# Two k multiplications moved to VectorE, the first expert's number found without a queue, row scatters begun a turn earlier

## The chip, the cores and the metric

The kernel runs on one core of a Trainium2 chip. The metric is the device time of one execution in microseconds (us); for the kernel before it is given as the median of three runs. The engines are TensorE (PE; its weight loads are PEld), VectorE (DVE), ScalarE (ACT), GpSimd (POOL) and the queue of SyncE (SP), which issues most DMAs. Each engine works through its own instructions in order.

## The reference

The computation is a gated linear attention followed by a mixture of experts, in float32. There are 4 sequences of 768 tokens, 8 heads of width 48, hence 3072 tokens of width 384.

```
f = sigmoid(f_logit)
for t in range(768):                                  # per sequence and head
    state = f[t][:, None] * state + outer(k[t], v[t])
    y[t] = q[t] @ state
x = y as 3072 rows of 384
e = argmax(x @ w_gate);  g = softmax(x @ w_gate)[e] * sigmoid(x @ w_output_gate)[e]
out = g * (relu(x @ w1[e]) @ w2[e])                   # 8 experts, hidden width 1024
```

## The kernel before, in words

**Attention in turns.** The recurrence is cut into chunks of 128 tokens: 4 sequences by 6 chunks give 24 chunks, worked off in 24 turns `t` (loop at line 465). Within a chunk the decay is turned into a running product p and its inverse i: `scan_p` (line 212) and `scan_i` (219) are scans along the chunk on VectorE. k is multiplied by i (`mul_k`, 223), q by p (`mul_q`, 226). Then the chunk is plain matrix work: `qk` (248) gives the scores of q and k, `mask` makes them causal, one half by a copy on ScalarE and a selection on POOL (253, 254), the other by a multiplication with a mask on VectorE (257); `out_y` (308, 312) adds what the state before the chunk gives and what the masked scores give; `state` (281) and `state_upd` (293 to 296) carry the state on. `evac_y` (319) copies the output out of PSUM as the tile xt, `x_tr` (325) transposes it and takes the gate logits along.

The turns overlap: turn `t` does the scores of chunk t, `mul_k` of chunk t + 1, the scans and `mul_q` of chunk t + 2, the output of chunk t - 1, and the copy, the transpose and the state update of chunk t - 2. `mul_k` and `mul_q` are POOL's, but for `mul_k` of the first three chunks, which is VectorE's (line 195). The order on each engine is that in which the loop issues the instructions; nothing sorts them afterwards.

**Routing beside it.** The 24 chunks of tokens fall into groups (four of 4, then four of 2). For each group `route` (367) puts eight small VectorE instructions into a list, `dq`; `fill` takes some from it at fixed places of each turn (eight a turn up to turn 19, more from turn 20), so that they stand between the large ones. When they are through, `slots` (406) runs with the next turn: a few small matmuls rank the tokens, and VectorE writes the slot of each token (419, 421). From turn 8 (`T_SCAT`, line 527) each turn ends with `scatter`: an indirect DMA, issued by POOL, that writes 128 token rows to their experts' slots in the buffer xs_dram; one a turn up to turn 19, up to four in turn 20. That buffer's upper slots are first cleared by eight SP DMAs (668); the first two scatters may overtake these, the later ones wait for them.

**The first expert.** After 16 chunks have been counted, in turn 19, `top` (392) finds the expert with the most tokens. Its first instruction (396) runs at once; the other six, the last of them the SP load of that expert's number and of its first weights (`ex.load`, 402, 403, 619), go to the front of `dq`: four of them come in turn 19, two in turn 20. When 16 row blocks have been scattered, at the end of turn 20, SP reads the first 256 rows of that expert back (`tokens_in`, 675) and then its second weights (634).

**Handing over.** In turn 22 the buffers of the early chunks are given up and the experts' weight tiles take their place (`done_sb.close()`, line 481). ScalarE and POOL begin to split the weights into a high and a low part (`split`, 649, 650). In turn 23 `x_early` (754) transposes the 256 early rows, after the last turn `mm1_early` (806) starts the expert, and then the eight experts follow one after the other, the largest first, with the next one's weights and rows loading beside them.

Of the kernel before, what the change touches and what calls it, by code (L numbers as in the profile page):

```python
# [14 lines left out]
ALU = mybir.AluOpType  # L15
AX = mybir.AxisListType
# [4 lines left out]
N, DM, E, F = B * S, H * D, 8, 1024  # L21
# [20 lines left out]
RW = LG + 2 * E  # L42
RG = (4, 4, 4, 4, 2, 2, 2, 2)
XW = 2 * D + 2 * E
T_SCAT = 8
HELD = 256
SB = 32
BW = DM // (128 // SB)
# [81 lines left out]
def attention(ctx, tc, nc, k, kpool, rt, q01, k01, f01, q23, k23, f23, v, wg, xs_dram, r, ex):  # L130
# [60 lines left out]
    def prep(ti):  # L191
        b, c = order[ti]
        i, sl, z = b % 2, slice(c * C, (c + 1) * C), ti % 2
        flat = lambda a: a.rearrange("p g t -> p (g t)")
        eng = nc.vector if ti < 3 else nc.gpsimd
        d = {}

        def s():
# [37 lines left out]
    def hot(t):  # L236
        return 0 <= t < len(order)
# [113 lines left out]
    dq, pq = [], []  # L351
# [40 lines left out]
    def top(ps):  # L392

        key = rt.tile([128, E], F32, name="key")
        mx = rt.tile([128, 1], F32, name="mx")
        nc.vector.scalar_tensor_tensor(out=key, in0=ps, scalar=float(E), in1=k.first_key, op0=ALU.mult, op1=ALU.add)
        dq[:0] = [
            lambda: nc.vector.tensor_reduce(out=mx, in_=key, axis=AX.X, op=ALU.max),
            lambda: nc.vector.tensor_tensor(out=r.top, in0=key, in1=mx.broadcast_to([128, E]), op=ALU.is_equal),
            lambda: nc.vector.tensor_tensor(out=key, in0=r.top, in1=k.num, op=ALU.mult),  # L400
            lambda: nc.vector.tensor_reduce(out=mx, in_=key, axis=AX.X, op=ALU.add),
            lambda: nc.vector.tensor_copy(out=r.top_id, in_=mx),
            lambda: ex.load(0, r.top_id[0:1, 0:1], rest=False),
        ]

    def slots(gi, t0, n):
        ts = slice(t0, t0 + n)
# [21 lines left out]
    for i in range(2):  # L429
        nc.sync.dma_start(out=turn[64 * i:64 * i + 64, 1::2, 2 * D:XW],  # L430
                          in_=wg[64 - 64 * i:128 - 64 * i, 1::2, 0:2 * E])
# [5 lines left out]
    def pre(t, *names):  # L437
        if hot(t):
            for nm in names:
                if nm not in done[t]:  # L440
                    done[t].add(nm)
                    pre_of[t][nm]()
# [8 lines left out]
    for g in range(2):  # L451
        for j in range(2):
            r0 = 64 * (j ^ g)
            nc.gpsimd.tensor_copy(out=turn[:, g::2, D * j:D * j + D],
                                  in_=k.ident[:, r0:r0 + D].unsqueeze(1).broadcast_to([128, 2, D]))
# [9 lines left out]
    for t in range(last + 1):  # L465
# [10 lines left out]
            state_upd(t - 2)  # L476
        if t == 2:
            pre(4, "f")
        pre(t + 1, "mul_k")
        if t + 1 == last:  # L480
            done_sb.close()
            ex.open_early()
        fill(more)
        if t > 1:
            pre(t + 2, "scan_p")
        qk(t)
        mask(t, 1)
        mask(t, 0)
        if t == 0:
            pre(2, "s", "f")  # L490
        pre(t + 2, "scan_p", "scan_i")
        if t == 0:
            pre(2, "mul_k")
# [24 lines left out]
        if t == last:  # L518
# [7 lines left out]
            ex.split(1, 0, 2, nc.gpsimd)  # L526
        if t >= T_SCAT:
            scatter(1 if t < T_END else 2)
# [701 lines left out]
```

## Time and profile before

| | |
|---|---|
| median of three runs | 366.68 us (364.68, 366.68, 368.03) |
| profiled execution | 361.12 us |
| its span, first to last instruction | 359.4 us |
| granted TensorE clock, mean | 1.000 of full speed |
| PE, DVE, ACT, POOL busy | 343.4, 259.4, 183.2, 146.8 us |

A row of a timeline gives the start in us from the span's start, the duration in us, the engine, the line, the instruction, output<-input, and in brackets how long the engine was idle before it and what released it. Rows of other views are explained where they stand. `L223` is line 223 of the kernel; SPq is the SP queue. The chunks' scores (L248) mark the turns: those of turn 21 start at 103.67 us.

### The profile page before, as it was taken

How to read it: one execution, taken by the hardware profiler on the slowest of the kernel's cores; microseconds unless marked ns; L12 is line 12 of the kernel's file. 1: busy time of each engine (PE TensorE's matmuls, PEld its weight loads, DVE VectorE, ACT ScalarE, POOL GpSimd, SP SyncE). 2: the span in 40 equal slices, each digit the busy share in tenths (PEclk: the TensorE clock that was granted, in tenths of full speed). 3: DMA queues.
4: the chain of work that ended last, by engine and by line, in shares of the span. 5: the costliest groups of instructions: out<-in, count | busy, mean ns of one | idle time of the engine just before them, and what ended most of it. 6: DMA issues, size and time to landing. Idle time of an engine off the chain costs nothing. (4 is left out here: it accounts for less than half of the span.)

```text
span 359.4 us, 8283 instructions
## 1 busy us (share of the span) xinstructions
PE 343.4 (96%) x3001; PEld 317.6 (88%) x3001; DVE 259.4 (72%) x517; ACT 183.2 (51%) x436; POOL 146.8 (41%) x176
## 2 busy tenths in 40 slices
PE   7889999999996999999999999999999999999994
PEld 2678898888896799997999899999999999999993
DVE  6998989898994665576685884975975974966610
ACT  3476776776763743455542453452552552464510
POOL 7586786999988853022000005004005005007112
PEclk9999999999999999999999999999999999999999
DMA  8999999999528714999458298399498499192101
GB/s 256 350 359 355 347 241 262 286 281 233 213 92 254 262 47 138 218 266 257 131 169 135 51 330 249 54 290 282 79 293 249 96 321 278 35 288 81 42 24 43
DMA packets 81458, 74.02 MB, mean 206 GB/s; under 512 B 37058, under 2 KB 76037, under 8 KB 81408
## 3 DMA queue, kind: packets, MB, share of 16 engines
q1 hardware_dynamic: 78096, 63.76, 63.8%
q0 software_dynamic: 3312, 9.65, 7.7%
q8 instruction: 25, 0.41, 0.5%
q14 instruction: 25, 0.20, 0.2%
HBM read 57.16 MB, written 16.68 MB: 205 GB/s over the span
## 5 line engine op out<-in xcount | busy, mean ns | idle before, releaser
L885 POOL DMA_INDIRECT out<-yr,dst x20 | 21.5, 1074 | 133.8 <-DMA yr<-yd 86.3
L810 ACT ACTIVATE hh<-h_ps 128x256 fp32r<-128x256 f32 (+6 forms) x72 | 34.8, 484 | 66.7 <-PE h_ps L806 65.2
L806 PE MATMUL h_ps<-xh,w1h 128*128 128x400 f32 (+6 forms) x192 | 66.9, 348 | 0.9 <-DVE hl L811 0.7
L811 DVE SCALAR_TENSOR_TENSOR hl<-h_ps,hh 128x256 fp32r<-128x256 f32 (+6 forms) x72 | 38.8, 540 | 37.8 <-ACT hh L810 37.2
L806 PE MATMUL h_ps<-xl,w1h 128*128 128x400 f32 (+6 forms) x192 | 65.1, 339 | 0.2 <-DVE xl L761 0.2
L806 PE MATMUL h_ps<-xh,w1l 128*128 128x400 f32 (+6 forms) x192 | 64.9, 338 | 0.0
L825 PE MATMUL y_ps<-hh,w2h 128*128 128x400 f32 (+3 forms) x120 | 42.2, 352 | 0.0
L825 PE MATMUL y_ps<-hh,w2l 128*128 128x400 f32 (+3 forms) x120 | 42.1, 351 | 0.0
L825 PE MATMUL y_ps<-hl,w2h 128*128 128x400 f32 (+3 forms) x120 | 42.1, 351 | 0.0
L806 PEld LDWEIGHTS h_ps<-xh,w1h 128*128 128x128 f32 x192 | 36.0, 188 | 6.3 <-DVE hl L811 4.7
L806 PEld LDWEIGHTS h_ps<-xl,w1h 128*128 128x128 f32 x192 | 36.1, 188 | 0.9 <-DVE xl L761 0.5
L806 PEld LDWEIGHTS h_ps<-xh,w1l 128*128 128x128 f32 x192 | 36.1, 188 | 0.4
L226 POOL TENSOR_TENSOR q_t<-q_t,p 128x512 f32<-128x512 f32 x24 | 30.6, 1274 | 8.4 <-DVE p L212 5.8
L248 PE MATMUL a_ps<-q_t,k_t 64*128 64x128 f32 x384 | 28.3, 285 | 5.8 <-POOL k_t L223 2.8
L650 DVE TENSOR_TENSOR w2l<-w2r,w2h 128x768 fp32r<-128x768 f32 x31 | 30.6, 989 | 3.5 <-ACT w2h L649 1.8
L248 PEld LDWEIGHTS a_ps<-q_t,k_t 64*128 64x128 f32 x384 | 23.6, 187 | 8.6 <-POOL k_t L223 3.4
L212 DVE TENSOR_TENSOR_SCAN p<-f_ps,start_p 128x511 f32<-128x511 f32 x22 | 28.0, 1274 | 3.7 <-ACT start_p L200 2.1
L650 DVE TENSOR_TENSOR w1l<-w1r,w1h 128x768 fp32r<-128x768 f32 x28 | 26.8, 956 | 3.5 <-ACT w1h L649 2.7
L223 POOL TENSOR_TENSOR k_t<-k_t,i 128x512 f32<-128x512 f32 x21 | 26.9, 1280 | 4.2 <-DVE i L219 2.7
L219 DVE TENSOR_TENSOR_SCAN i<-f_ps,start_i 128x512 f32<-128x512 f32 x22 | 26.9, 1223 | 0.8
L325 PE MATMUL x_ps<-turn,xt 128*128 128x112 f32 x192 | 25.7, 277 | 1.7 <-ACT xt L319 1.7
L649 ACT CAST w1h<-w1r 128x768 fp32r<-128x768 f32 x32 | 26.0, 834 | 2.3 <-POOL k_t L223 2.3
(175 smaller groups left out, 764.2 us busy)
## 6 DMA issues: line engine op xcount, KB each, us to landing
w1r<-in_w SPq DMA_DIRECT2D x32, 384.0 KB, 5.1
w2r<-in_w SPq DMA_DIRECT2D x32, 384.0 KB, 4.5
xs_dram<-empty SPq DMA_DIRECT2D x8, 401.0 KB, 9.7
f_t<-in_f SPq DMA_DIRECT2D x6, 512.0 KB, 7.2
q_t<-in_q SPq DMA_DIRECT2D x6, 512.0 KB, 8.9
k_t<-in_k SPq DMA_DIRECT2D x6, 512.0 KB, 9.6
v_t<-in_v SPq DMA_DIRECT2D x6, 512.0 KB, 8.7
v_t<-in_v SPq DMA_DIRECT2D x4, 768.0 KB, 14.2
```

What stands on the lines that cost most here:

```text
L212: nc.vector.tensor_tensor_scan(out=flat(d["p"])[:, 1:n], data0=flat(d["f"])[:, 0:n - 1], data1=sp[:, 1:n], initial=sp[:, 0:1], op0=ALU.mul ...
L219: nc.vector.tensor_tensor_scan(out=flat(d["i"])[:, ::-1], data0=flat(d["f"])[:, ::-1], data1=flat(k.start_i[z])[:, ::-1], initial=0.0, op0 ...
L223: eng.tensor_tensor(out=k_t[i][:, :, sl], in0=k_t[i][:, :, sl], in1=d["i"], op=ALU.mult)
L226: nc.gpsimd.tensor_tensor(out=q_t[i][:, :, sl], in0=q_t[i][:, :, sl], in1=d["p"], op=ALU.mult)
L248: nc.tensor.matmul(aps[t][par][:, g, :], k_t[b % 2][r, g, sl], q_t[b % 2][r, g, sl], start=(g == 0), stop=(g == NP - 1))
L325: nc.tensor.matmul(xps[t][:, g, :], xt[t][:, g, :], turn[:, g, :], start=(g == 0), stop=(g == NP - 1))
L649: self.nc.scalar.copy(out=flat(hi), in_=raw)
L650: (eng or self.nc.vector).tensor_tensor(out=flat(lo), in0=raw, in1=flat(hi.bitcast(F32)), op=ALU.subtract)
L806: nc.tensor.matmul(ps[:, 0:n], a[:, c, cs], b, start=(i == 0), stop=(i == 3 * KC - 1))
L810: nc.scalar.activation(out=hi, in_=ps[:, 0:n], func=AF.Relu)
L811: nc.vector.scalar_tensor_tensor(out=lo, in0=ps[:, 0:n], scalar=0.0, in1=hi.bitcast(F32), op0=ALU.max, op1=ALU.subtract)
L825: self.nc.tensor.matmul(self.yps[d][:, 0:n], a[:, d, fs], b, start=(f == 0 and i == 0), stop=(f == KF - 1 and i == 2), skip_group_check=True)
```

## The change

Three edits. From `T_VEC` = 22 on, `mul_k` (of chunks 22 and 23, issued in turns 21 and 22) is VectorE's, and it is issued behind the turn's mask instead of ahead of the scores; in those turns the forward scan is issued behind it too. In `top` the six instructions no longer go through `dq` but follow at once, so they stand ahead of the slot computation of the same group. `T_SCAT` becomes 7.

```diff
@@ -42,7 +42,8 @@
 RW = LG + 2 * E
 RG = (4, 4, 4, 4, 2, 2, 2, 2)
 XW = 2 * D + 2 * E
-T_SCAT = 8
+T_SCAT = 7
+T_VEC = 22
 HELD = 256
 SB = 32
 BW = DM // (128 // SB)
@@ -192,7 +193,7 @@
         b, c = order[ti]
         i, sl, z = b % 2, slice(c * C, (c + 1) * C), ti % 2
         flat = lambda a: a.rearrange("p g t -> p (g t)")
-        eng = nc.vector if ti < 3 else nc.gpsimd
+        eng = nc.vector if ti < 3 or ti >= T_VEC else nc.gpsimd
         d = {}
 
         def s():
@@ -394,14 +395,12 @@
         key = rt.tile([128, E], F32, name="key")
         mx = rt.tile([128, 1], F32, name="mx")
         nc.vector.scalar_tensor_tensor(out=key, in0=ps, scalar=float(E), in1=k.first_key, op0=ALU.mult, op1=ALU.add)
-        dq[:0] = [
-            lambda: nc.vector.tensor_reduce(out=mx, in_=key, axis=AX.X, op=ALU.max),
-            lambda: nc.vector.tensor_tensor(out=r.top, in0=key, in1=mx.broadcast_to([128, E]), op=ALU.is_equal),
-            lambda: nc.vector.tensor_tensor(out=key, in0=r.top, in1=k.num, op=ALU.mult),
-            lambda: nc.vector.tensor_reduce(out=mx, in_=key, axis=AX.X, op=ALU.add),
-            lambda: nc.vector.tensor_copy(out=r.top_id, in_=mx),
-            lambda: ex.load(0, r.top_id[0:1, 0:1], rest=False),
-        ]
+        nc.vector.tensor_reduce(out=mx, in_=key, axis=AX.X, op=ALU.max)
+        nc.vector.tensor_tensor(out=r.top, in0=key, in1=mx.broadcast_to([128, E]), op=ALU.is_equal)
+        nc.vector.tensor_tensor(out=key, in0=r.top, in1=k.num, op=ALU.mult)
+        nc.vector.tensor_reduce(out=mx, in_=key, axis=AX.X, op=ALU.add)
+        nc.vector.tensor_copy(out=r.top_id, in_=mx)
+        ex.load(0, r.top_id[0:1, 0:1], rest=False)
 
     def slots(gi, t0, n):
         ts = slice(t0, t0 + n)
@@ -476,18 +475,22 @@
             state_upd(t - 2)
         if t == 2:
             pre(4, "f")
-        pre(t + 1, "mul_k")
+        late = t + 1 >= T_VEC
+        if not late:
+            pre(t + 1, "mul_k")
         if t + 1 == last:
             done_sb.close()
             ex.open_early()
         fill(more)
-        if t > 1:
+        if t > 1 and not late:
             pre(t + 2, "scan_p")
         qk(t)
         mask(t, 1)
         mask(t, 0)
         if t == 0:
             pre(2, "s", "f")
+        if late:
+            pre(t + 1, "mul_k")
         pre(t + 2, "scan_p", "scan_i")
         if t == 0:
             pre(2, "mul_k")
```

## Rows read from the trace of the kernel before

**Rows 1.** The page, busy time, share and instructions of each engine
```profile
PE 343.4 (96%) x3001; PEld 317.6 (88%) x3001; DVE 259.4 (72%) x517; ACT 183.2 (51%) x436; POOL 146.8 (41%) x176
```

**Rows 2.** Windows view, 105 to 125 us: length, then busy us of each engine
```profile
105.00:125.00 20.00, 16.44 (x257) 14.04 (x256) 11.62 (x37) 11.00 (x27) 17.13 (x18) 1.00 0.78 254
```

**Rows 3.** TensorE's timeline, turns 21 to 23: start, us, instruction, idle before it
```profile
103.67 1.16 PE L248 MATMUL a_ps<-q_t,k_t 64*128 64x128 f32 x16
110.48 1.16 PE L248 MATMUL a_ps<-q_t,k_t 64*128 64x128 f32 x16 [1.94 <-POOL k_t L223]
116.06 1.16 PE L248 MATMUL a_ps<-q_t,k_t 64*128 64x128 f32 x16 [0.88 <-POOL k_t L223]
117.47 1.15 PE L325 MATMUL x_ps<-turn,xt 128*128 128x112 f32 x8 [0.25 <-ACT xt L319]
120.70 0.63 PE L754 MATMUL x_ps<-ident,first_x 128*128 128x128 f32 x4
```

**Rows 4.** POOL's timeline, turns 19 to 22
```profile
99.95 1.01 POOL L342 DMA_INDIRECT xs_dram<-xn,slot  x1 [0.17 <-issue]
100.99 1.28 POOL L223 TENSOR_TENSOR k_t<-k_t,i 128x512 f32<-128x512 f32 x1
108.15 0.98 POOL L342 DMA_INDIRECT xs_dram<-xn,slot  x1 [0.30 <-issue]
109.14 1.28 POOL L223 TENSOR_TENSOR k_t<-k_t,i 128x512 f32<-128x512 f32 x1
114.73 1.28 POOL L223 TENSOR_TENSOR k_t<-k_t,i 128x512 f32<-128x512 f32 x1
```

**Rows 5.** Source view, line 223 on VectorE: count, ns min/median/max, first and last
```profile
L223 DVE TENSOR_TENSOR k_t<-k_t,i x3: 692/692/1040, 8.4 to 15.5; 128x512 f32<-128x512 f32 x3
```

**Rows 6.** VectorE's timeline, turns 19 to 22
```profile
99.55 0.19 DVE L421 TENSOR_REDUCE slot<-rk 128x4 int32<-128x32 f32 x1
103.70 0.13 DVE L402 CAST top_id<-mx 128x1 int32<-128x1 f32 x1
107.15 0.66 DVE L257 TENSOR_TENSOR at<-a_ps,mask 128x512 f32<-128x512 f32 x1
109.74 0.36 DVE L296 TENSOR_TENSOR state<-misc,pend 128x192 f32<-128x192 f32 x1
```

**Rows 7.** ScalarE's timeline, turn 22
```profile
109.26 0.37 ACT L319 COPY xt<-two_ps 128x256 f32<-128x256 f32 x1 [0.46 <-DVE rk L419]
```

**Rows 8.** SP queue's timeline, first token read of expert 0
```profile
115.18 0.37 SPq L675 DMA_DIRECT2D first_x<-xs_dram  x1
```

**Rows 9.** DMA view, 100 to 130 us: issues, KB each, us to landing
```profile
first_x<-xs_dram SPq DMA_DIRECT2D x1, 401.0 KB, 4.0
```

**Rows 10.** VectorE's timeline, turn 7
```profile
45.54 0.19 DVE L421 TENSOR_REDUCE slot<-rk 128x4 int32<-128x32 f32 x1
```

**Rows 11.** POOL's timeline, turn 10
```profile
59.50 1.27 POOL L226 TENSOR_TENSOR q_t<-q_t,p 128x512 f32<-128x512 f32 x1 [2.57 <-DMA q_t<-in_q]
```

**Rows 12.** TensorE's weight loads, timeline, turn 14
```profile
72.00 0.97 PEld L248 LDWEIGHTS a_ps<-q_t,k_t 64*128 64x128 f32 x16 [0.18 <-POOL k_t L223]
```

**Rows 13.** DMA view, 40 to 70 us: queue, packets, MB, share of 16 engines
```profile
q0 software_dynamic: 192, 0.62, 6.2%
```

**Rows 14.** VectorE's timeline, 124 to 137 us
```profile
125.02 1.99 DVE L650 TENSOR_TENSOR w2l<-w2r,w2h 128x768 fp32r<-128x768 f32 x1
135.19 0.96 DVE L650 TENSOR_TENSOR w2l<-w2r,w2h 128x768 fp32r<-128x768 f32 x1 [0.30 <-ACT w2h L649]
```

**Rows 15.** POOL's timeline, 120 to 137 us
```profile
124.33 1.85 POOL L650 TENSOR_TENSOR w1l<-w1r,w1h 128x768 fp32r<-128x768 f32 x1
134.94 0.98 POOL L342 DMA_INDIRECT xs_dram<-xn,slot  x1 [0.30 <-issue]
```

**Rows 16.** Tile view of the clearing writes: issues, and time to landing
```profile
L668 SPq DMA_DIRECT2D xs_dram<-empty x8: 372/686/1049, 32.5 to 39.9; - x8
DMA to landing us min/median/max: 9.2/9.7/12.2
```

## The prediction

> **What bounds the kernel now.** The page comes first: TensorE is busy 96% of the span and POOL 41% [rows 1]. A mean over stages does not price an edit in one stage, so the second view is the window in which the change ends, 105 to 125 us. There TensorE is busy 16.44 of 20 us and POOL 17.13 [rows 2]: 3.56 us of TensorE idle lie here, and that is the most that these edits can take out of this stretch. TensorE's timeline names the waits [rows 3]. The scores of turn 22 start at 110.48 after 1.94 us of idle, those of turn 23 at 116.06 after 0.88 us, both released by POOL's multiplication of k (line 223); the transpose of turn 21's output at 117.47 waits 0.25 us for xt. POOL's timeline says why k is late [rows 4]: POOL does nothing wrong, it is simply queued up. The last of turn 20's four scatters starts at 108.15, the multiplication of k of chunk 22 directly behind it at 109.14, that of chunk 23 at 114.73. From then on TensorE has work nearly without a gap, so what arrives earlier there should end earlier.
>
> **Moving the last two multiplications.** POOL loses two instructions of 1.28 us [rows 4]; VectorE gains two at 0.69 us, the usual duration of the same line in the first turns, at most 1.04 [rows 5]. Is k ready in time there? The forward scan of chunk 23 now stands behind the mask and the multiplication, so the mask of turn 21, which began at 107.15 behind that scan [rows 6], begins about 1.2 us sooner, at 105.96, and k of chunk 22 is done at about 105.96 + 0.6 + 0.69 = 107.25. TensorE could start that turn's scores at 110.48 - 1.94 = 108.54 [rows 3], so the whole 1.94 us go. Everything that follows on VectorE in turn 21 is 0.6 us later: the state update that began its last step at 109.74 and took 0.36 [rows 6] ends at 110.7 instead of 110.1. Behind it come the mask (0.6, its input long there) and the second multiplication (0.69): k of chunk 23 is done at about 112.0. Its scores want it at 116.06 - 1.94 - 0.88 = 113.24, so the 0.88 us go as well, and so does the 0.25 us of 117.47: xt was late there because ScalarE sat behind a weight cast that waited for POOL's multiplication.
>
> What is late next: ScalarE's copy of xt at 109.26 was held until VectorE's rank multiplication of that turn was over [rows 7]. That one is 0.6 us later now, so xt is there near 110.3, while TensorE is through with the transposes of k at about 110.1. I charge 0.25 us. Sum of this part: 1.94 + 0.88 + 0.25 - 0.25 = 2.82 us gained.
>
> **The expert's number in one go.** Five small VectorE instructions, about 0.2 us each by the slot reduction's 0.19 [rows 6], stand ahead of the ranks of turn 19 instead of behind them; only the cast (0.13) truly moves, from 103.70 to about 100.3, so VectorE's total is the same. The slots of that group, ready at 99.55 + 0.19 = 99.74 [rows 6], are ready at about 100.7. That costs POOL a wait, because turn 19's scatter is now the first row block of just this group: it starts at about 100.9 instead of 99.95 [rows 4]. Behind it in POOL's queue stands k of chunk 21 (100.99 before), now done at about 103.2; TensorE wants it at 103.67 [rows 3]. Cost nothing, with 0.45 us to spare; if the wait is longer than that, the rest is lost. On the SP queue the expert's weights start some 3.3 us sooner, into DMA engines that were nearly idle then, and nothing else stands behind them in that queue until turn 20 ends.
>
> **Scatters from turn 7.** The number of scatters is the same, 24, each one place earlier, so three instead of four stand in turn 20. POOL's last one there is 0.93 later by the wait above and one step of 0.98 + 0.30 = 1.28 us earlier [rows 4]: start 107.8 instead of 108.15. The read of the early tokens waits for it. That read went out at 115.18 [rows 8] and took 4.0 us [rows 9], so tokens lay at 119.2, and the transposes that use them began at 120.70 [rows 3]. With TensorE 2.8 us earlier they begin at 117.9, and the tokens would be late if nothing moved. But the scatters then shared the DMA engines with the expert's weights; these are now 3.3 us ahead. I put the read near 112 and the tokens near 116: covered.
>
> At the front the extra scatter of turn 7 must wait for its slots (45.54 + 0.19 [rows 10]), so POOL starts it near 45.9, just where the multiplication for the next turn stood; POOL then runs about 1.3 us late for three turns. That is hidden: POOL sits 2.57 us at 59.50 anyway, waiting for a load of q [rows 11]. The load itself is the cost. Up to 72.00, where TensorE's weight load of the scores waits for POOL's k [rows 12], POOL works from that load without a rest, so what delays the load delays TensorE. A scatter costs the 16 DMA engines 6.2% of 30 us over three of them, 0.62 us each [rows 13], in a stretch in which they are full, and about one scatter more now goes ahead of that load. Bounds: 0, if it slips into idle engines, and 1.24, if both of the first two go ahead of it. A gain isn't to be had, since the load has no less ahead of it. I take 0.6, one scatter.
>
> **The sum.** 2.82 - 0.6 = 2.2 us off. The profiled execution took 361.12 us (its span of 359.4 and 1.7 around it), so its like would take 358.9. The runs' median, 366.68, lies 5.56 us above that execution; the gain is a difference inside the span, so I take it off the median: 364.5 us, 0.6% less.
>
> **A rule against it.** The trace shows that a VectorE instruction with both inputs in SBUF can be held by POOL: a subtraction of 0.96 us [rows 14] took 1.99 when a POOL subtraction had begun before it and ran to 126.18 [rows 14, 15]. Beside a POOL scatter it does not: the one at 135.19 took 0.96 although a scatter ran until 135.92 [rows 14, 15]. The new multiplications have both inputs in SBUF, and by POOL's queue only scatters run beside them, so I charge nothing. The Trainium skill, page "SBUF — State Buffer", section "Who interferes with whom", states that such an instruction and a GpSimd instruction that reads SBUF exclude each other for a whole instruction; the trace agrees (1.99 against 0.96), and if it held for scatters too, each multiplication could come a scatter late and the result would be the third rival's.
>
> **Rivals.**
> - *Nothing lost at the front, and the stretch closes up* (0.16). For it: later turns have slack on POOL. Against it: the 0.18 us wait at 72.00. The bound is all 3.56 us of idle: 363.1.
> - *The early tokens are the new wait* (0.08). If their read goes out after 113.9 instead of 112, TensorE waits for them. At worst they lie where they lay, 119.2, and 1.3 of the 2.2 us are given back: 365.8.
> - *VectorE becomes the bound of turns 21 to 23* (0.14). It carries 1.4 us more there. If a multiplication is held by a POOL scatter or multiplication (about 1 us), everything behind it, rank and xt among them, is 1 us later and xt's wait grows by as much: 365.5.
> - *The third scatter waits for the clearing writes* (0.05, slower than before). Only the first two may overtake them; the third moves from turn 10 to turn 9, near 54.8. The last clear was issued at 39.9 and the longest landing is 12.2, so 52.1 at worst in this execution [rows 16]. Were it later, POOL would stand with k of chunk 11 queued behind the scatter. Of the 2.57 us that POOL has to spare at 59.50 [rows 11], 1.3 are used by turn 7's wait, so TensorE loses what goes beyond 54.8 + 1.3 = 56.1, and the gain is used up from a landing at 58.3. A landing at 62 gives a loss of 3.7: 370.4.
> - *The change does not do what it says* (0.07): the scores of turn 22 find another releaser at the same time, q of that chunk or the score buffers, both on engines just as full. No change: 366.7.
>
> The forecast has the remaining 0.50.
>
> **How the numbers follow.** About 1% (3.7 us) is what a measurement of this kernel can tell from no change; the runs shown spread from 364.68 to 368.03. Faster by over 1% means below 363.0. The forecast gets there by scatter of the median alone (about 0.18 of its cases), the first rival in half of its cases, the others seldom: 0.09 + 0.08 + 0.03 = 0.20. Slower by over 1% (above 370.3) is the rival of the clearing writes and a little of the rest: 0.06. Within 1%: 0.74. The range reaches from 0.9 us below the first rival, for the scatter of the runs, to just above the case of no change: 362.2 to 367.0. The slower rival and the tails of the others are left out.
>
> **What the trace after would show.** Right: the k multiplication five times on VectorE, the last two near 107 and 111; scores of turns 22 and 23 without a wait for k; the cast of the expert's number about 3 us earlier; the first scatter near 46; the first token read near 112. Wrong: a wait of over 0.5 us before the scores of turn 21, before the token transposes, or TensorE more than 1 us later at turn 15 than before; or a POOL scatter in turn 9 released by the clearing writes.

## The result, and the profile after

The whole change takes **360.86 us** (median; 359.25 to 361.26) where the kernel before, measured beside it, takes 365.0 us (362.85 to 368.03, the three runs shown among them): ratio 0.989, 95% interval 0.986 to 0.992. The forecast was 364.5, with a range from 362.2 to 367.0. The sign is right; the change is worth 4.1 us instead of 2.2, and the time lies below the range. Medians and ranges, here and below, are of all runs; the ratios and their intervals leave out runs over 1.5% above the fastest of the same kernel, and can differ from the quotient of the medians by a few tenths of a percent.

One thing is odd at once. The profiled execution of after took 361.26 us, its slowest run, and that of before 361.12, faster than any of its timed runs. The two profiled executions differ by 0.1 us, the medians by 4. So two questions stand: does the late stretch win what was forecast, and what do the ordinary executions of the kernel before lose that its profile does not show?

The page of after and its window from 105 to 125 us answer to [rows 1] and [rows 2]:

```profile
PE 344.4 (96%) x3001; PEld 317.9 (88%) x3001; DVE 260.7 (73%) x519; ACT 183.3 (51%) x436; POOL 144.4 (40%) x174
```

```profile
105.00:125.00 20.00, 19.06 (x304) 16.51 (x305) 14.97 (x45) 12.20 (x31) 16.66 (x18) 1.00 0.73 251
```

Two instructions have gone from POOL to VectorE, and TensorE is busy 19.06 of 20 us instead of 16.44. Its timeline in turns 21 to 23, against [rows 3]:

```profile
106.35 1.16 PE L249 MATMUL a_ps<-q_t,k_t 64*128 64x128 f32 x16
111.88 1.16 PE L249 MATMUL a_ps<-q_t,k_t 64*128 64x128 f32 x16
116.51 1.16 PE L249 MATMUL a_ps<-q_t,k_t 64*128 64x128 f32 x16
117.60 1.15 PE L326 MATMUL x_ps<-turn,xt 128*128 128x112 f32 x8
120.84 0.63 PE L757 MATMUL x_ps<-ident,first_x 128*128 128x128 f32 x4
```

The waits of 1.94, 0.88 and 0.25 us have gone. (One of 0.39 us is new, at 111.73 ahead of a rank matmul; the profile names no releaser for it, and e8, e11 and e12 below do not have it.) From the scores of turn 21 to the token transposes it takes 14.49 us instead of 17.03: 2.54 us won. But turn 21 itself starts 2.68 us later than before (106.35 against 103.67), which eats it. POOL's and VectorE's timelines, against [rows 4] and [rows 6], and the source view of line 224 on VectorE, against [rows 5]:

```profile
46.11 1.22 POOL L343 DMA_INDIRECT xs_dram<-xn,slot  x1 [1.17 <-DVE state L294]
...
54.97 1.01 POOL L343 DMA_INDIRECT xs_dram<-xn,slot  x1 [0.17 <-issue]
...
103.18 1.01 POOL L343 DMA_INDIRECT xs_dram<-xn,slot  x1 [1.50 <-DVE state L294]
104.22 1.29 POOL L224 TENSOR_TENSOR k_t<-k_t,i 128x512 f32<-128x512 f32 x1
```

```profile
101.84 0.17 DVE L399 TENSOR_TENSOR top<-key,mx 128x8 f32<-128x8 f32 x1
102.04 0.17 DVE L400 TENSOR_TENSOR key<-top,num 128x8 f32<-128x8 f32 x1
...
102.43 0.15 DVE L402 CAST top_id<-mx 128x1 int32<-128x1 f32 x1
...
102.72 0.19 DVE L420 TENSOR_REDUCE slot<-rk 128x4 int32<-128x32 f32 x1
...
109.00 0.68 DVE L224 TENSOR_TENSOR k_t<-k_t,i 128x512 f32<-128x512 f32 x1
...
113.79 0.68 DVE L224 TENSOR_TENSOR k_t<-k_t,i 128x512 f32<-128x512 f32 x1
```

```profile
L224 DVE TENSOR_TENSOR k_t<-k_t,i x5: 682/693/1042, 8.4 to 113.8; 128x512 f32<-128x512 f32 x5
```

The SP queue, against [rows 8]:

```profile
103.64 2.18 SPq L622 DMA_DIRECT2D w1r<-in_w  x4
113.67 0.37 SPq L678 DMA_DIRECT2D first_x<-xs_dram  x1
```

Two k multiplications stand on VectorE, at 109.00 and 113.79, and the read of the early tokens goes out 7.3 us behind the start of turn 21 instead of 11.5. The step to read is at 103.18 on POOL: POOL's scatter of turn 19 now waits 1.50 us, where before it went at once [rows 4]. The profile names the state update as what released it, but it starts 0.27 us behind the end of its slots (102.72 + 0.19 on VectorE), and in each of the six further profiles with scatters from turn 7 it starts 0.27 or 0.28 us behind them: it waits for the slots. The 2.7 us that turn 21 is late come from the front (2.2 us) and from turn 20 (0.5 us). These are TensorE's two largest waits at the front, at turns 12 and 13, and a copy of ScalarE in turn 20:

```profile
64.88 1.23 PE L249 MATMUL a_ps<-q_t,k_t 64*128 64x128 f32 x16 [0.60 <-POOL k_t L224]
...
72.71 0.44 PE L313 MATMUL two_ps<-at,v_t 128*64 128x128 f32 x4 [0.90 <-DMA v_t<-in_v]
```

```profile
102.77 0.37 ACT L320 COPY xt<-two_ps 128x256 f32<-128x256 f32 x1 [0.59 <-DVE rk L418]
```

TensorE waits for a k of POOL and for a load of v that both came in time in the profile of before. In turn 20 ScalarE's copy of xt waits for VectorE's rank multiplication, which now stands behind the small instructions of the expert's number.

### The profile page after: what moved, and what is told of

Read it like the earlier page. It is cut to its first block, busy times and chain, and to the rows that moved or that the text cites. A ratio compares the mean times of both kernels' runs of the same rounds, so it can differ in the third digit from the quotient of the medians.

```text
span 359.6 us, 8283 instructions
## 1 busy us (share of the span) xinstructions
PE 344.4 (96%) x3001; PEld 317.9 (88%) x3001; DVE 260.7 (73%) x519; ACT 183.3 (51%) x436; POOL 144.4 (40%) x174
## 5 line engine op out<-in xcount | busy, mean ns | idle before, releaser
L343 POOL DMA_INDIRECT xs_dram<-xn,slot x24 | 24.2, 1010 | 7.7 <-issue 3.8
L838 PE MATMUL y_ps<-w2h,hh 128*128 128x384 f32 (+1 forms) x80 | 27.1, 339 | 0.0
```

The lines of the kernel that those rows point to most:

```text
L343: i = nc.gpsimd.indirect_dma_start(out=xs_dram, out_offset=bass.IndirectOffsetOnAxis(ap=r.slot[:, t:t + 1], axis=0), in_=xn[t // 4][:, t % ...
L838: self.nc.tensor.matmul(ps[0:n, 0:DM], a, b[:, f % 2, :], start=(f == 0 and i == 0), stop=(f == KF - 1 and i == 2))
```

## The experiments

Each ratio is to the kernel before, measured beside the run (medians of before: 363.2 for e1 to e4, 363.3 for e5 to e8, 363.0 for e9 to e12, 364.6 for e13 to e15). "Turn 20" is the time between the scores of turns 20 and 21 in the profile, 4.63 us where nothing waits, as before (99.04 to 103.67). "Held" is explained below.

| run | scatters from | multiplications / number | median us (range) | ratio, 95% | v late | held | turn 20 |
|---|---|---|---|---|---|---|---|
| e1 | 8 | POOL / queue | 363.1 (361.7 to 367.5) | 1.000 [0.996, 1.004] | no | no | 4.64 |
| e2 | 8 | VectorE / queue | 360.5 (358.9 to 363.2) | 0.993 [0.990, 0.996] | 0.83 | yes | 5.83 |
| e3 | 8 | POOL / in one go | 363.1 (361.7 to 366.8) | 1.000 [0.996, 1.005] | 1.53 | yes | 6.85 |
| e4 | 7 | POOL / queue | 361.2 (360.0 to 362.4) | 0.994 [0.991, 0.997] | no | no | 4.64 |
| e5 | 7 | VectorE / queue | 359.4 (358.6 to 363.5) | 0.991 [0.988, 0.994] | 0.78 | no | 4.63 |
| e6 | 8 | VectorE / in one go | 361.1 (358.9 to 364.5) | 0.993 [0.990, 0.997] | 1.69 | yes | 8.40 |
| e7 | 8 | e2, PSUM operands | 362.4 (361.2 to 364.2) | 0.998 [0.995, 1.001] | 1.73 | no | 4.63 |
| e8 | 7 | whole change, v early | 361.1 (359.4 to 362.7) | 0.993 [0.990, 0.996] | no | no | 5.12 |
| e9 | 8 | e6, PSUM operands | 361.5 (361.1 to 365.2) | 0.996 [0.993, 1.000] | no | no | 5.35 |
| e10 | 8 | e6, v early | 360.0 (358.5 to 363.9) | 0.993 [0.989, 0.997] | no | yes | 8.35 |
| e11 | 7 | e5 again | 358.9 (358.4 to 360.7) | 0.989 [0.984, 0.993] | no | no | 4.64 |
| e12 | 7 | whole change again | 359.6 (359.2 to 366.2) | 0.989 [0.983, 0.994] | 1.04 | no | 5.14 |
| e13 | 8 | e6, VectorE 0.4 later | 366.5 (362.6 to 370.4) | 1.002 [0.998, 1.006] | no | yes | 8.41 |
| e14 | 7 | whole change, VectorE 0.4 later | 360.0 (359.8 to 361.3) | 0.988 [0.983, 0.993] | no | no | 5.52 |
| e15 | 8 | before, VectorE 0.4 later | 364.9 (363.9 to 366.4) | 1.002 [1.000, 1.005] | no | yes | 5.94 |

**The kernel before, again (e1).** No edit.

> The kernel before, unchanged, for a second profile. Its profiled execution so far (361.12 us) is faster than each of its six timed ones (362.85 to 368.03, median 365.0). Theory 1, a wait that comes and goes: a second execution near 365 shows TensorE idle some 3 to 4 us longer in one stretch than the first profile, and it is the stretch of turns 8 to 15, where the DMA engines are full and loads land late. Theory 2: the excess is at turns 20 to 23, the first tokens read back too late, and the first token read goes out after 117. Theory 3: the excess is spread over the whole span, or lies outside it, and no stretch differs by over 1 us.

Its runs spread over 5.8 us, with a tail to 367.5, and its profiled execution is again its fastest run (361.65), so it decides between none of the three theories. It shows no wait for v, and TensorE's wait for k is there (1.78 us at 110.66). Behind that wait TensorE's granted clock fell from 1.00 to 0.50, the lower of its two levels (1.2 instead of 2.4 GHz), and stayed there from about 111 to 114.5 us; turn 22 took 6.22 us instead of 5.58. The profile of before has a wait as long (1.94 us) and no such fall. One profile of this kernel is no picture of its median.

**One edit at a time (e2, e3, e4).** The multiplications alone (with their place in the order), the number alone, the scatters alone:

```diff
# e2
-        eng = nc.vector if ti < 3 else nc.gpsimd
+        eng = nc.vector if ti < 3 or ti >= T_VEC else nc.gpsimd
...
# e3
-        dq[:0] = [
-            lambda: nc.vector.tensor_reduce(out=mx, in_=key, axis=AX.X, op=ALU.max),
...
+        nc.vector.tensor_reduce(out=mx, in_=key, axis=AX.X, op=ALU.max)
...
# e4
-T_SCAT = 8
+T_SCAT = 7
```

> Only the last two k multiplications on VectorE behind the mask; the queue of small instructions and the scatters as before. By the prediction's terms this part is worth 2.8 us (ratio 0.992) and the waits of 1.94 and 0.88 us for k in turns 22 and 23 are gone. Theory 2 of the run before (tokens read back late) wants less here, since the read of the tokens isn't earlier: under 1.5 us (0.996 or above), with a wait before the token transposes.

> Only the first expert's number found in one go. By the prediction: no gain and no loss (ratio 1.000 within 0.003), since the waits for k in turns 22 and 23 stay; weights of the first expert issued near 101.6 instead of 104.9. If the weights' earlier start is what takes the load off the scatters and the token read (theory 2), the ratio is 0.996 or less.

> Only the scatters from turn 7. By the prediction: TensorE loses 0.6 us (0 to 1.24) at turns 10 to 14, and gains up to 1.28 us at turn 22 since three scatters instead of four stand ahead of its k multiplication: together 0.7 us faster (ratio 0.998). If the early scatter brings nothing in the front and the gain at turn 22 stays, 0.9965; if the front loses what the two profiles differ by there (2.7 us), 1.004 or above.

e2 wins 0.73% (2.7 us): the late part of the forecast. e3 wins nothing. e4 wins 2.1 us, where the forecast had a loss of 0.6 for this edit beside the others, and the expectation a gain of 0.7 for it alone. Part of that is plain in TensorE's timeline of e4:

```profile
109.28 1.16 PE L248 MATMUL a_ps<-q_t,k_t 64*128 64x128 f32 x16 [0.72 <-POOL k_t L223]
```

With one scatter less ahead of it in turn 20, POOL's k of chunk 22 comes 1.2 us sooner (0.72 us of wait instead of 1.94). Beside the VectorE multiplications, where no wait for k is left, this part has nothing more to win. The rest of e4's gain shows in its spread, 2.4 us (ten runs) against 6.6 for the kernel before (31 runs) beside it. And e2 and e3 show what their own executions lost in turn 19. For comparison, these are the two instructions in the profile of before, and then the timeline of VectorE and POOL in e2, with the wait of TensorE that follows:

```profile
99.84 0.17 DVE L399 TENSOR_TENSOR top<-key,mx 128x8 f32<-128x8 f32 x1
100.04 0.17 DVE L400 TENSOR_TENSOR key<-top,num 128x8 f32<-128x8 f32 x1
```

```profile
100.31 1.01 POOL L343 DMA_INDIRECT xs_dram<-xn,slot  x1 [0.17 <-issue]
...
100.81 1.86 DVE L400 TENSOR_TENSOR top<-key,mx 128x8 f32<-128x8 f32 x1
101.35 1.29 POOL L224 TENSOR_TENSOR k_t<-k_t,i 128x512 f32<-128x512 f32 x1
102.58 0.65 POOL L255 TENSOR_SCALAR_AFFINE_SELECT at<-at 128x512 f32<-128x512 f32 x1
102.71 0.54 DVE L401 TENSOR_TENSOR key<-top,num 128x8 f32<-128x8 f32 x1
...
103.77 0.33 PE L309 MATMUL two_ps<-q_t,state 64*64 64x128 f32 x2 [1.12 <-DVE state L294]
```

An instruction of eight columns takes 1.86 us instead of 0.17, and the next one 0.54. The first ends at 102.67, when POOL's multiplication ends (101.35 + 1.29 = 102.64); the second at 103.25, when POOL's selection ends (103.23). That is the hold: these two read both inputs from SBUF, as POOL's instructions do, and end with them. Everything behind them on VectorE, the state update among it, is late.

The Trainium skill, page "SBUF — State Buffer", section "Who interferes with whom", states that a VectorE instruction with two SBUF inputs and a GpSimd instruction that reads SBUF exclude each other for a whole instruction. The trace agrees in this: 0.17 us becomes 1.86, to the end of POOL's instruction. That the held instruction had begun 0.54 us before that of POOL stays open (below).

**Theory A** was then: the kernels with scatters from turn 8 run into this hold in part of their executions, and scatters from turn 7 exclude it, because POOL's scatter of turn 19 then needs the slots of just the group that VectorE works out beside these two instructions, so POOL's multiplication behind that scatter cannot come too early. With the number found in one go the slots come behind the two. With the queue they come just ahead of them, and the scatter still keeps its distance, as in the timeline of VectorE and POOL in e11:

```profile
99.53 0.19 DVE L422 TENSOR_REDUCE slot<-rk 128x4 int32<-128x32 f32 x1
...
99.82 0.17 DVE L400 TENSOR_TENSOR top<-key,mx 128x8 f32<-128x8 f32 x1
100.00 1.01 POOL L343 DMA_INDIRECT xs_dram<-xn,slot  x1 [0.47 <-DVE top L400]
100.02 0.17 DVE L401 TENSOR_TENSOR key<-top,num 128x8 f32<-128x8 f32 x1
```

The scatter starts 0.28 us behind the end of the slots, and POOL's multiplication a scatter later, at 101.03, when the two are over. Rival B: the hold only goes along with something else (late loads, the pace of a stage).

**Two edits at a time (e5, e6).** e5 is the change without the number in one go, e6 the change with `T_SCAT = 8`.

> The multiplications on VectorE and the scatters from turn 7, the small instructions of the expert's number still queued. Theory A (POOL's hold): in turn 19 two tiny VectorE instructions with both inputs in SBUF (lines of top: is_equal and the product with num) are held by POOL's k multiplication when POOL is early relative to VectorE (1.86 and 1.90 us instead of 0.17 in the two profiles with a late load of v, 0.17 in the others); with the scatters from turn 7, POOL's scatter of turn 19 waits for the slots of just this group, so the two can't meet. Then this kernel is as fast as the whole change: ratio 0.989 (0.987 to 0.991), runs within 3 us of each other, both instructions at 0.17 us. Rival B (the expert's number in one go is needed for the rest): 0.9925, as with the multiplications alone.

> The whole change but for the scatters, which start in turn 8 again. Theory A: POOL's scatter of turn 19 no longer waits for the slots, the tiny instructions can be held, and now the slots stand behind them, so a held run loses more: ratio 0.992 to 0.996, runs spread over 4 us or more. Rival B: 0.989 as the whole change. Rival C (the early scatter helps by itself, by fewer scatters in turn 20 or in the front): 0.9925, with the spread of the multiplications alone.

e5 is as fast as the whole change (0.991 against 0.989). Its runs spread further than expected, though: nine lie at 358.6 to 360.6, two at 362.5 and 363.5. These two have the lowest mean granted clocks (0.991 and 0.988, the others 0.995 to 0.998), and no profile shows what made them long. e6 falls into two clusters, 358.9 to 360.0 (five runs) and 361.1 to 364.5 (six). Its profiled execution is its longest and was held: turn 20 took 8.40 us, though e3, held as long and with the same wait of TensorE behind it (1.95 us), took 6.85. The difference is the clock. In the windows view (length, busy us of each engine, and third from the end the granted clock), first e6 and then e3, behind that wait:

```profile
106.50:109.00 2.50, 2.50 (x29) 1.97 (x30) 2.43 (x6) 1.09 (x5) 2.26 (x3) 0.50 0.75 231
```

```profile
105.50:108.00 2.50, 2.50 (x48) 2.22 (x47) 2.47 (x4) 1.65 (x7) 2.01 (x3) 1.00 0.43 130
```

In e6 the granted clock fell to the 1.2 GHz level soon after TensorE had begun to work again, and the same matmuls took longer (two of the output's first matmuls, line 309, 0.42 us instead of 0.28). It did so in e10 and e13 below too, whose turn 20 also took some 8.4 us, and not in e2, e3 and e15. Against the turn 20 of kernels that were not held (4.63 us with the queue, 5.1 with the number in one go), the hold alone costs 1.2 to 1.7 us there, and with the fall of the clock behind it some 3.2.

**No two SBUF inputs (e7, e9).** The key and a copy of the numbers lie in a bank of PSUM, in e2's kernel and in e6's:

```diff
-        key = rt.tile([128, E], F32, name="key")
+        key, num = misc[:, 400:400 + E], misc[:, 416:416 + E]
...
+        nc.vector.tensor_copy(out=num, in_=k.num)
```

> The multiplications on VectorE alone, scatters from turn 8, number queued; but the key and a copy of the numbers 0 to 7 lie in PSUM, so that neither of the two tiny instructions has both inputs in SBUF (one more VectorE copy of about 0.13 us). Theory A: they can't be held any more, and what the early scatter adds is had without it: ratio 0.989 to 0.990, both instructions near 0.17 us in the profile. Rivals B and C: 0.9925, as with the multiplications alone.

> The whole change with scatters from turn 8 (as in the run vec_top), but the key and a copy of the expert numbers lie in PSUM, so that neither of the two eight-column instructions of the first expert's number has two SBUF inputs. Theory A (POOL's k multiplication of turn 19 holds these instructions whenever TensorE and VectorE have fallen behind POOL): the upper of the two clusters of that run (362.5 to 364.5) empties, each of the two instructions takes 0.17 us in the profile whether or not v came late, and the median goes to 359.5 to 360.5. Rival B (the long runs come from the late loads or from the pace of the expert stage, the hold is only a sign of them): the median and the spread stay as in that run, 361 and 359 to 364.5, although no instruction is held.

The mechanism is confirmed, the time is not. In e7's timeline the second of the two runs inside POOL's multiplication, and the first 0.17 us ahead of it, without being held:

```profile
103.14 0.17 DVE L401 TENSOR_TENSOR top<-misc,mx 128x8 f32<-128x8 f32 x1
103.31 1.29 POOL L224 TENSOR_TENSOR k_t<-k_t,i 128x512 f32<-128x512 f32 x1
103.34 0.17 DVE L402 TENSOR_TENSOR misc<-top,misc 128x8 f32<-128x8 f32 x1
```

Turn 20 takes 4.63 us though v came 1.73 us late. But both kernels lose time far behind the change: set beside those of before, matmul for matmul, their records drift apart by 2.0 us between 170 and 250 us, without any wait that the trace names. The groups view of 172 to 245 us (count, busy us, mean ns of one, idle before) has the 432-wide matmuls longer; in e9:

```profile
L829 PE MATMUL y_ps<-hh,w2h 128*128 128x432 f32 x24 | 8.7, 362 | 0.0
```

The same group takes 356 ns in the kernel before, at a granted clock of 1.00 in both. So the expected 0.990 was missed for a reason that has nothing to do with turn 19 and stays open, and these runs alone do not settle A against B.

**v loaded early (e8, e10).** The first half of v goes directly behind f, ahead of k and q; in the whole change and in e6's kernel:

```diff
-            load(b + 2, [("fkq", c, c + 3)])
-            if c:
-                load(b + 2, [("v", 0, 3), ("v", 3, NCH)])
+            load(b + 2, [("f", c, c + 3), ("v", 0, 3), ("kq", c, c + 3), ("v", 3, NCH)] if c else [("fkq", c, c + 3)])
```

> The whole change, and the loads issued at turns 6 and 12 in another order: the first half of v directly behind f, ahead of k and q. In three of six profiles TensorE waits 0.83 to 1.53 us in turn 13 for v. Theory D: this wait, which comes and goes, is what is left of the difference between runs; without it the median falls by 0.3 to 0.9 us: ratio 0.987 to 0.988, fastest run unchanged. Rival: k and q, now behind v, land late in its place, and the ratio stays at 0.989 or rises.

> The whole change with scatters from turn 8, and the first half of v loaded directly behind f, ahead of k and q. The two tiny instructions stay open to a hold. Theory A with late v as what sets the two engines back: without the wait for v they begin within 0.25 us of POOL's scatter and are not held (0.17 us each); the upper cluster empties and the median is 359.5 to 360.5. Rival B (something other than v decides how far VectorE is behind POOL in turn 19): holds of 1.9 us are still there in the profile or the times still reach 362.5 and above in a third of the runs, median near 361.

The wait for v has gone in both, and no time with it. e8 even stands at 0.993, where the whole change has 0.989 twice; nothing is held in its profile, so the reason is another, and it is open. Against e10 (0.993 as well, though measured in another set), scatters from turn 7 win nothing here. e10 refutes the idea that late v is what opens the hold. Its timeline of VectorE and POOL:

```profile
100.03 1.01 POOL L343 DMA_INDIRECT xs_dram<-xn,slot  x1 [0.17 <-issue]
...
100.31 0.17 DVE L399 TENSOR_TENSOR top<-key,mx 128x8 f32<-128x8 f32 x1
100.51 1.87 DVE L400 TENSOR_TENSOR key<-top,num 128x8 f32<-128x8 f32 x1
101.07 1.27 POOL L224 TENSOR_TENSOR k_t<-k_t,i 128x512 f32<-128x512 f32 x1
```

The first of the two, 0.28 us behind the scatter's start, runs free; the second, at 0.48, is held to the end of the multiplication (102.38 against 102.34). In the profiles of e2, e3 and e6 the held ones began 0.50, 0.44 and 0.45 us behind the scatter's start; in the two of the kernel before none began later than 0.25, and none was held. Counted to POOL's multiplication, instructions that began up to 0.60 us before it were held, those that began 0.76 us or more before it were free. A few tenths of a microsecond decide, and e10's times still fall into two clusters (358.5 to 360.0 six times, 361.8 to 363.9 five times).

**The hold forced (e13, e14, e15).** The first instruction of the number runs three times over, which puts the two instructions 0.4 us later against POOL: in e6's kernel, in the whole change, in the kernel before.

```diff
-        nc.vector.scalar_tensor_tensor(out=key, in0=ps, scalar=float(E), in1=k.first_key, op0=ALU.mult, op1=ALU.add)
+        for _ in range(3):
+            nc.vector.scalar_tensor_tensor(out=key, in0=ps, scalar=float(E), in1=k.first_key, op0=ALU.mult, op1=ALU.add)
```

> The whole change with scatters from turn 8, and the first instruction of the expert's number three times over (two more of 0.14 us, 0.2 us apart), so that the two tiny two-input instructions begin 0.4 us later against POOL's scatter of turn 19. They began 0.28 and 0.48 us behind that scatter's start in the last profile, the second held. Theory A (the hold, decided by a few tenths of a microsecond): now they begin 0.45 to 0.9 us behind it in every execution, every execution is held, and the lower of the two clusters of this kernel (358.4 to 360.0, half of its runs) is empty: all runs at 361 to 365, median near 362.7. Rival B (the two clusters have another cause): both clusters stay, the lower one moved by no more than the 0.4 us that the two instructions take, median 360 to 361.5.

> The whole change as it is (scatters from turn 7) with the same two extra instructions. Theory A: POOL's scatter of turn 19 waits for the slots that come behind the two instructions, so they cannot be held: 0 to 0.4 us more than the whole change (359.6 to 361.3), the two instructions 0.17 us each in the profile. Rival B: the same loss as in the kernel with scatters from turn 8.

> The kernel before with the same two extra instructions. In its two profiles the two tiny instructions began -0.1 to +0.25 us from the scatter's start and were not held; now they begin at +0.3 to +0.65. Theory A, if the long runs of the kernel before (363.5 to 368) are held ones: one or both are held in the profile, 1.9 us, and the lower half of its runs (361.5 to 363) thins out: median 363.8 to 365. Rival B: within 0.4 us of the kernel before.

This settles A against B for the kernel with the number in one go, by e13 against e14. e13 has lost its lower cluster: one run at 362.6, all others above 365, ratio 1.002 instead of 0.993. (It lost more than the 361 to 365 that was expected; the kernel before was 1.5 us longer beside it too, but that does not cover it. In its profile the clock fell behind the hold, and turn 21 took 6.32 us where e6 took 4.80, with another wait of 1.07 us at 111.50.) VectorE, POOL and TensorE in e13:

```profile
101.09 1.70 DVE L400 TENSOR_TENSOR top<-key,mx 128x8 f32<-128x8 f32 x1
101.49 1.27 POOL L224 TENSOR_TENSOR k_t<-k_t,i 128x512 f32<-128x512 f32 x1
...
103.99 1.15 PE L326 MATMUL x_ps<-turn,xt 128*128 128x112 f32 x8 [2.16 <-ACT xt L320]
```

e14, the same delay with scatters from turn 7, loses nothing (0.988), since POOL waits along:

```profile
99.94 0.17 DVE L400 TENSOR_TENSOR top<-key,mx 128x8 f32<-128x8 f32 x1
100.14 0.17 DVE L401 TENSOR_TENSOR key<-top,num 128x8 f32<-128x8 f32 x1
...
101.28 1.01 POOL L343 DMA_INDIRECT xs_dram<-xn,slot  x1 [1.71 <-DVE state L294]
```

The kernel before, so delayed (e15), is held as well:

```profile
103.42 1.29 POOL L223 TENSOR_TENSOR k_t<-k_t,i 128x512 f32<-128x512 f32 x1
103.43 1.89 DVE L400 TENSOR_TENSOR top<-key,mx 128x8 f32<-128x8 f32 x1
104.66 0.64 POOL L254 TENSOR_SCALAR_AFFINE_SELECT at<-at 128x512 f32<-128x512 f32 x1
```

Its lower edge moves from 362.2 (21 runs) to 363.9 (11 runs), its median hardly (364.9 against 364.6). The median by itself fits both theories; that a forced hold leaves it where it was fits a kernel most of whose executions were held already in that set of runs. No profile of the unchanged kernel before caught one, so for that kernel the hold is possible and not shown. There are rivals: the profile of e15, its longest run, lost 2.1 us in turns 16 to 18 as well, in waits for xt of 0.41, 0.96 and 0.35 us that come before the hold. With the number still queued (e2 against e5 and e11) the profiles agree with A, but no pair was forced.

**The change without its second edit and the whole change, side by side (e11, e12).** e11 is e5's kernel again, e12 the whole change again.

> The change without its second edit (the number still found through the queue), a second time, beside the whole change. If the second edit is worth nothing by itself: the same median as the whole change within 0.3% (1 us). If the first reading of this kernel (359.4) was no accident of one call: 359 to 360, and 0.3 to 0.5% under the whole change.

> The whole change, unchanged. By its first measurement 360.9 (359.3 to 361.3). Theory A: with scatters from turn 7 POOL's multiplication of turn 19 comes behind the two instructions in every run, so there is no upper cluster: all runs within 2.5 us. Rival B: the spread is no narrower than that of the two kernels with scatters from turn 8 above.

358.9 against 359.6, with intervals that overlap, as e5 did with the first measurement of the change: the second edit gives nothing by time. (One of e12's five runs took 366.2 us, against the expectation of a spread within 2.5 us, at a mean granted clock of 0.986, the others 0.995 to 1.000.) By the profiles it costs about 0.5 us in turn 20 (5.12 to 5.14 us in after, e8 and e12, 4.63 and 4.64 in e5 and e11) and gives it back: from the scores of turn 21 to the token transposes it takes 14.00 us in e8 and e12, 14.76 and 14.64 in e5 and e11. In e11 nothing came late at the front and nothing was held, so it is the execution to set against the profile of before. TensorE's timeline in e11, against [rows 3]:

```profile
103.66 1.16 PE L249 MATMUL a_ps<-q_t,k_t 64*128 64x128 f32 x16
...
108.45 1.16 PE L249 MATMUL a_ps<-q_t,k_t 64*128 64x128 f32 x16
...
110.42 1.15 PE L326 MATMUL x_ps<-turn,xt 128*128 128x112 f32 x8 [0.22 <-ACT xt L320]
...
118.30 0.63 PE L759 MATMUL x_ps<-ident,first_x 128*128 128x128 f32 x4 [0.26 <-ACT xt L320]
```

Turn 21 starts where it did before (103.66 against 103.67), the tokens' transposes 2.40 us sooner, and the profiled execution takes 358.41 us, 2.71 less than that of before.

## Why the prediction was right or wrong

**The moved multiplications: right, to a few tenths.** Set against the start of turn 21, after's k of chunk 22 is done at 109.68 - 106.35 = 3.33 and that of chunk 23 at 114.47 - 106.35 = 8.12, in the clock of before 107.0 and 111.8; forecast 107.25 and 112.0. All three waits went, and the new wait for xt that was charged with 0.25 is there in e11 with 0.22. The term of 2.82 us measures 2.54 in after, 2.40 in e11's late stretch, and 2.7 (0.73%) in the times of e2.

**The rule on two SBUF inputs: right rule, wrong instructions.** It was weighed for the moved multiplications only, and these are not held (0.68 us each in after, beside scatters). The same edit list touches two instructions of eight columns with both inputs in SBUF, and they stand close to POOL's multiplication in turn 19. I did not ask what runs beside *them*: the profile of before shows them at 0.17 us, free by a few tenths.

**The number in one go, "cost nothing, with 0.45 us to spare": right in sum, wrong in what it weighed.** The places are right. Set against the start of turn 20 (101.23 in after, 99.04 before), in the clock of before, the cast is at 100.2 (forecast 100.3), POOL's scatter at 101.0 (100.9), and k of chunk 21 done at 103.3 (103.2). What I did not see is ScalarE's copy of xt, which waits 0.59 us for the rank multiplication (the wait that I charged with 0.25 in turn 22); turn 20 gets about 0.5 us longer, and turns 21 to 23 give it back. But the wait of POOL for the slots, which I took for a cost that happens to be hidden, is where a second gain of the change can lie. It comes from `T_SCAT = 7` alone (e4 and e11 have it without the second edit) and it keeps POOL's multiplication off the two instructions. With scatters from turn 7 none of seven profiles shows the hold; with scatters from turn 8 and two SBUF inputs the unchanged kernel's two do not, all six others do (two of them forced). Its size is known only roughly: e6 and e10 stand at 0.993, the whole change at 0.989 twice, so some 0.4%, 1.5 us, but the intervals overlap, and e8, which has scatters from turn 7, stands at 0.993 too.

**The front, -0.6: not borne out.** The parts are right: the first scatter at 46.11 (forecast 45.9), the third at 54.97 without waiting for the clears (54.8), and POOL's 2.57 us of slack [rows 11] shrinks to 1.29 in e11. But the load is not later for it as a rule. The multiplication of q that waited for it, at 59.50 before, starts at 59.20 to 61.00 in the seven profiles with the early scatter, and at 58.91 to 60.75 in the ten without it. Against the profile of before, TensorE loses at most 0.1 us between turns 10 and 14 in e4, e8, e11 and e14, with the early scatter, 1.2 and 1.3 in e5 and e12 and 2.1 in after; without it, at most 0.1 in e1, e9 and e10, and 0.5 to 2.5 in the others, most of it waiting for v in e2, e3, e6 and e7. Late loads come and go whatever `T_SCAT` is. My test "TensorE over 1 us later at turn 15" did come out in after (78.82 against 76.63), and it says nothing about the change.

**The term for the scatters and the base: the steps that failed.** The time came out 3.6 us below the forecast, 1.9 of it in the gain and 1.7 in the base; either alone would have stayed inside the range (362.8 and 362.5). In the gain the failed term is that of the scatters from turn 7. I put it at -0.6 us, a delayed load at the front, and wrote that a gain was not to be had. The runs show no such loss, and a gain instead. By the ratios, the multiplications alone win 2.7 us (e2), with the scatters added it is 3.3 and 4.2 (e5, e11), so the scatters give 0.6 to 1.5, though these intervals overlap; the whole change wins 4.0 and 4.1 (the result and e12; by the medians 4.1 and 3.4). What the early scatter does there is to hold POOL back until its slots are ready, so that the hold of turn 19 cannot happen; e13 against e14 shows this for the kernel with the number in one go, with 1.4% between them. Whether the median of the kernel before contained the hold, and what share of these 0.6 to 1.5 us the hold is, is not shown. In the base, I took a gain "inside the span" off a median that lay 5.56 us above the profiled execution, without asking what the other executions had more. 366.68 was the median of three runs out of a long tail, 365.0 that of six, about 363 to 364.6 later. That two misses of the same sign met is chance.

**The rivals.** None of them came in as a whole. Of the first, one half did: nothing was lost at the front to the early scatter; but the stretch did not close up: 2.54 of its 3.56 us were won. The tokens were not the new wait (their read went out at 113.67, in the clock of before 111.0, forecast 112), the third scatter did not wait, VectorE did not become the bound of turns 21 to 23, and the change did what it says.

**What stays open.** Why an instruction is held that begins 0.4 to 0.6 us before POOL's multiplication does, while POOL is still at its scatter; whether the long runs of the kernel before were held, and which of them; why TensorE's clock fell behind a wait of 1.78 to 2.16 us in e1, e6, e10 and e13 and not behind 1.94 and 1.95 us in before and e3; why e8 is slower than the whole change; why the matmuls of e7 and e9 took some 5 ns longer between 170 and 250 us; what makes v late in some executions.

## What to carry to other kernels

When one profiled execution is faster than every timed run, ask what the others have more before taking a difference off the median: a change can be worth more in the executions that no trace shows. Look through *all* small VectorE instructions with two SBUF inputs for the POOL work that they could meet within 0.6 us, not only through the ones that are moved; their own 0.17 us says nothing of what they cost when held. A wait between two engines can be a gain: here it ties POOL to VectorE, so that their order no longer depends on a few tenths of a microsecond. And look at the granted clock behind a wait: in e6 the fall behind the hold cost about as much as the hold.

## What the runs showed of the hardware that was not expected

- An eight-column VectorE instruction with two SBUF inputs took 1.70 to 1.90 us instead of 0.17 beside a POOL multiplication of 1.28 us, and turn 20 of TensorE grew to 5.83 us (e2) and 6.85 (e3) from 4.63, and to 8.35 to 8.41 (e6, e10, e13) where the clock fell as well. With one input in PSUM it took 0.17 us while the same multiplication ran (e7).
- The hold also took instructions that began during the indirect DMA ahead of the multiplication, 0.44 us or more behind its start (e2, e3, e6, e10, e13); those that began up to 0.28 us behind it were free (before, e1, e10). The scatter by itself held nothing: the second moved multiplication began 0.65 us into a scatter in after (113.79, the scatter at 113.14), with another scatter and not a multiplication next in POOL's queue, and took its 0.68 us.
- One held instruction can outlast two POOL instructions: in e15 it began 0.01 us behind the multiplication and ended at 105.32, when the selection behind it ended (105.30).
- TensorE's granted clock fell from 1.00 to 0.50 (1.2 instead of 2.4 GHz) for 3.2 to 3.5 us after it had stood idle for 1.9 to 2.2 us and begun to work again (e6, e10, e13; e1 after 1.78 us), and stayed at 1.00 after 1.94 and 1.95 us (before, e3).
- The same matmul group took 356 ns in the kernel before and 362 ns in e7 and e9, at a granted clock of 1.00.
